# Account of engine time in a scheduled kernel: a task is ready when its predecessor has ended, new first values, one ScalarE square fewer, another order at the end

## The chip, the cores and the metric

The kernel runs on one core of a Trainium2 chip. The metric is the device time of one execution in microseconds (us), as the median of several runs. The engines are named as in the profile: PE (TensorE, matrix products), DVE (VectorE), ACT (ScalarE), POOL (GpSimd), SP (SyncE, which here only starts transfers). Each works through its own instructions in their order and waits on the others by semaphores.

## The reference

Three stages in a row, on 6080 tokens of width 256:

```python
# 1: channel attention; q, k, v are 6080 x 256
s = (k / norm(k)).T @ (q / norm(q)) / tau      # 256 x 256, norms over the tokens
x = v @ softmax(s)
# 2: a feed-forward layer, d_ff = 2048
x = (relu(x @ moe_w_in) ** 2) @ moe_w_out
# 3: another
h = x @ moe2_w_in
out = (h * clip(h + 3, 0, 6) / 6) @ moe2_w_out
```

The weights arrive as 64-bit floats and are turned into 32-bit ones on the chip.

## The kernel before, in words

**Tiling.** Tokens lie along the free axis, in 6 chunks of about 2 x 508. After the attention scores (to about 55 us) a loop runs over 2 layers (`ph`) x 6 chunks (`c`) x 4 cuts of d_ff (`u`) x 2 halves of a cut (`p`), 96 steps `i` of about 10.3 us each (`step`, called from the loop at the end of the function). A step forms a 2 x 2 block product with seven products M1 to M7 in place of eight (Winograd's form). Operands are split into a rounded part and a rest ("hi" and "lo", tiles `wh`/`wl` for weights, the two halves of `b` for data, of `g` for the activations), so each product is three matmuls of 128 x 128 by about 506 columns.

**PE's order within a step** is fixed by `step`: M1, M2, M5 (nine matmuls), 3 of the previous step's 24 output matmuls (`out_mms`, line 765), M6, 5 more, M7, 6 more, M4, 5 more, M3, and the last 5: 45 matmuls. M1, M6, M7 and M4 add up in one PSUM bank `x`, and between them ScalarE copies the bank out: to `m1` after M1, `u2` after M6, `u3` after M7, and after M4 a relu to `r`. So M6 cannot start before the copy to `m1` is done, M7 not before `u2`, M4 not before `u3`. M3 adds into the bank that DVE has to read for `h22 = u3 + y`, and waits for that. From these come h11, h12, h21, h22; each is squared by DVE (or, for some steps, by ACT: relu and square, table `SQUARED_BY_ACT`), then ACT makes the hi half of `g` and DVE the lo half. h12's square and split (`carry`) run in the next step.

**Work on the side.** In layer 1 the weights of layer 2 are prepared as `tasks`: 64-bit words are converted (`ct`, `cv` by ACT; `ct`, `wblk` by DVE, line 138 the last of four), and a task marked `alone` (`add_in_2`, `part`) splits them: ACT writes the hi part to a staging tile `st`, DVE the lo part, and SP stores both to DRAM. A `lane` prepares the data blocks `b` of the next chunk.

**What sets the order.** PE, SP and POOL run in the order written. For ACT and DVE, from step 8 (`MANUAL_FROM`) on, an account of engine time does it while the program is built: `now` holds a time for PE, ACT and DVE; every emitted instruction adds its cost from a table (`MATMUL`, `WIDE_ACT`, `WIDE_DVE`, ...). Between the fixed parts of a step `fill(act_until, dve_until)` emits those side instructions that by the account start early enough to end by then, the earliest first. `starts` takes a task's first instruction as ready at `t.seen`. That is set when the task is loaded, to PE's time plus `LANDING` (3 us), and again whenever one of its own instructions is emitted. The account runs from the kernel's start: `run_outs` adds to PE's time in the first 8 steps too, where `step`'s fixed work is not charged to ACT and DVE.

**The end.** After the last step 24 output matmuls remain, then copies of four results `y` out of PSUM (`y_done`), the last one cut in halves for ACT and DVE. They are run 12 first (with the two copies that these complete), then `carry` (the last square and split of h12), then the other 12.

Of the kernel before, what the change touches and what calls it, by code (L numbers as in the profile page):

```python
# [8 lines left out]
F32 = mybir.dt.float32  # L9
# [7 lines left out]
P = 128  # L17

HALF = 256
HT = 508  # L20
# [26 lines left out]


MATMUL, SEEN, AFTER = 0.2305, 0.26, 0.12
WIDE_ACT, WIDE_DVE, SCALAR_DVE, HALF_ACT, HALF_DVE = 0.55, 0.6, 0.46, 0.32, 0.31  # L50
LANDING = 3.0
LOAD_AHEAD = (2, 8, 8)
PLAIN = 3
# [6 lines left out]
POPS_2 = (3, 5, 6, 5)  # L60
AW_POPS = (1, 1, 1, 1)
FIRST_POPS = (6, 7, 4, 7)
SQUARED_BY_ACT = ("1", "012", "1", "012", "12", "12", "12", "012")


@with_exitstack
def tile_channel_attention_then_two_ffn(
# [13 lines left out]
    PE, ACT, DVE, SP = nc.tensor, nc.scalar, nc.vector, nc.sync  # L81
# [17 lines left out]
    mp = ctx.enter_context(tc.tile_pool(name="mp", bufs=1))  # L99
# [110 lines left out]
    def run(fs):  # L210
        for f in fs:
            f()


    tasks = []
# [8 lines left out]
    def ensure_loads():  # L224
        for t in tasks[:2]:
            if t.steps is None:
                t.steps, t.since, t.seen = t.load(), done[0], now["PE"] + LANDING
# [16 lines left out]
    now = {"PE": 0.0, "A": 0.0, "D": 0.0}  # L244
    lane_seen, stagings = [0.0], [0.0, 0.0]

    def on(engine, cost, f, waits=False, staging=0):
        f.on, f.waits, f.staging = (engine, cost), waits, staging
        return f

    def spend(engine, cost, ready=0.0):
        now[engine] = max(now[engine], ready) + cost
        return now[engine] + AFTER
# [5 lines left out]
    def spent(f, seen):  # L259
        end = spend(*f.on, starts(f, seen))  # L260
        if f.staging == 2:
            stagings.append(end + LANDING)
        return end
# [6 lines left out]
    def emit(k):  # L270
        t = tasks[k]
        turn[0] = k
        f = t.steps.pop(0)
        f()
        t.seen = spent(f, t.seen)
        done[0] += 1
        if not t.steps:
            finished.add(tasks.pop(k).name)
            turn[0] = 0
            ensure_loads()  # L280

    def background(n=1):
        while n > 0 and tasks:
# [88 lines left out]
    def late(make, fine):  # L372

        got = []
        costs = [("A", WIDE_ACT)] * 2 + [("D", SCALAR_DVE)] * 2 + [("D", WIDE_DVE)] * 2
        if not fine:
            costs = [(e, 2 * cost) for e, cost in costs[::2]]

        def at(i):
            def f():  # L380
                if not got:
                    got.extend(make())
                got[i]()
            return on(*costs[i], f, i in (0, len(costs) // 3))
        return [at(i) for i in range(len(costs))]

    for u in range(NU):
        pool, tag = (gp, "g") if u == 0 else (oop, "oh")
# [182 lines left out]
    with tc.tile_pool(name="qk", bufs=4) as qkp, tc.tile_pool(name="at", bufs=1) as atp:  # L571
# [51 lines left out]
        for i, (wide, j, g) in enumerate(pieces):  # L623
            if i:
                load_piece(i + 3)
            t = loaded[i]
# [151 lines left out]
    def y_done(ph, c, b, e, last=False):  # L778
        start, n = chunks[c]
        if ph == 0 and c not in scratch:  # L780
            scratch[c] = dram.tile([C, 2 * HT], F32, tag="y1", name="y1")
        scale = 1.0 if ph == 0 else 1.0 / 6.0


        if ph == 0 and b == 0 and c == NCHUNK - 1:
            pool, tag, bufs = mp, ("u3", "h22")[e], 1
        else:
            pool, tag, bufs = (mp, "r", 2) if ph == 0 and b == 0 else (yp, "y", 2)
        t = pool.tile([P, HT], F32, tag=tag, name="y", bufs=bufs)
        y = y_ps[ph, c, b, e]  # L790
        dst = scratch[c][:, b * n:] if ph == 0 else outT[:, start + b * n:]
        dst = dst[e * P:(e + 1) * P]
        cuts = (0, n // 2, n) if last else (0, n)
        for k, (i, j) in enumerate(zip(cuts, cuts[1:])):
            if k:
                DVE.tensor_scalar(out=t[:, i:j], in0=y[:, i:j], scalar1=scale, scalar2=None, op0=ALU.mult)
            else:
                ACT.activation(out=t[:, i:j], in_=y[:, i:j], func=AF.Copy, scale=scale)
            spend("A", WIDE_ACT, now["PE"] + SEEN)
            (nc.gpsimd if ph == 0 else ACT if last and not k else SP).dma_start(out=dst[:, i:j], in_=t[:, i:j])  # L800

    def run_outs(outs, n):
        for _ in range(min(n, len(outs))):
            f, done = outs.pop(0)
            f()
            now["PE"] += MATMUL
            if done:
                y_done(*done)

    def step(i, ph, c, u, p, before, outs, carry):  # L810
# [35 lines left out]
        def act(h, b):  # L846
            if i < len(SQUARED_BY_ACT) and b in SQUARED_BY_ACT[i]:
                r = tmp("r", 2)
                ACT.activation(out=r, in_=h, func=AF.Relu)
                ACT.activation(out=h, in_=r, func=AF.Square)  # L850
            elif ph == 0:
                DVE.scalar_tensor_tensor(out=h, in0=h, scalar=0.0, in1=h, op0=ALU.max, op1=ALU.mult)  # L852
            else:
                r = tmp("r", 2)
                DVE.tensor_scalar(out=r, in0=h, scalar1=3.0, scalar2=0.0, op0=ALU.add, op1=ALU.max)  # L855
                DVE.scalar_tensor_tensor(out=h, in0=r, scalar=6.0, in1=h, op0=ALU.min, op1=ALU.mult)  # L856

        def relu2(h, x, k):
            r = tmp("r", 2)
            ACT.activation(out=r, in_=x, func=AF.Relu)  # L860
            if str(k) in SQUARED_BY_ACT[i]:
                ACT.activation(out=h, in_=r, func=AF.Square)
# [232 lines left out]
    for i, (ph, c, u, p) in enumerate(order):  # L1095
        at = i % (LAST + 1)
        nxt = (ph, c + 1) if c + 1 < NCHUNK else (1, 0) if ph == 0 else None
        if ph == 0 and c == 0:
            if i == 0:
                add_out_1(1, 3)  # L1100
            elif p == 1 and u + 1 < NU and u:
                add_out_1(u + 1, i + 2)
        if i == 1:
            need(("half o", 0))
            last_lo[2] = last_lo[0].ins
            held.extend([("s", 0), ("w", 0, 1)])
        if (ph, c) == (0, 1) and at == 0:
            end = i + 2
            for x, f in [(x, f) for x in range(NU) for f in (add_in_2, add_out_2)]:
                end += DUE[f is add_out_2]  # L1110
                f(x, end)
        if nxt and at == (2 if i > LAST else 6):
            add_lane(*nxt, FIRST if i > LAST else FIRST + REST, i - at + LAST + (i <= LAST))
        if at == 0:
            assert not lane
        if ph == 0:
            need(("w", ph, u))
            if PLAIN <= u and c == 0:
                need(("t", 0, 0))
            if c == 1 and u < PLAIN:  # L1120
                need(("s", u))
        outs = []
        if not prev:
            need(("w1", 1))
            take = take_next
            outs = [(f, None) for f in ahead[1:]]
        else:
            if prev[0][0] == 0 and prev[0][1] == 0:
                if i > 1:
                    need(("o", prev[0][2]))  # L1130
            outs = out_mms(*prev[0], prev[1])
        if i == MANUAL_FROM:
            phase[0] = 2
            ctx.enter_context(tc.manual_schedule())

        if nxt and at == LAST < i:
            add_lane(*nxt, REST, i + 1)
        g, carry = step(i, ph, c, u, p, before, outs, carry)
        if i == 1:
            first_hi = last_lo[1]  # L1140
        before = []
        if nxt and at == (0 if i > LAST else 5):
            if i <= LAST:
                need(("t", 0, 0))
            load_data(*nxt)
        if ph == 0 and c == 0 and p == 0 and u + 1 < NU:
            need(("w1", u + 1))
            if u:
                if u + 1 == SPLIT_FROM:
                    with tc.issue_after(first_hi), tc.issue_after(last_lo[2]):  # L1150
                        split_e()
                products, before = attn_w(u + 1)
                run(products)
            else:
                before = take
            add_task(("w", 0, u + 1), lambda x=u + 1: in_1_steps(x), i + 2)
        if ph == 0 and c == 0 and u < PLAIN:
            if p == 0 and u == PLAIN - 1 < NU - 1:
                add_data("t", 0, 0, ("sums", 5, 4, 3, 6), i + 2)
            elif p == (u < NU - 1):  # L1160
                add_weight_sums(u, SUMS_DUE[u])
        if ph == 0 and c == NCHUNK - 1 and p:
            fetch_2("w", u)
        if prev and prev[0][0] == 0 and prev[0][1] == NCHUNK - 1 and prev[0][3]:
            fetch_2("o", prev[0][2])
        prev = ((ph, c, u, p), g)
    outs = out_mms(*prev[0], prev[1])
    run_outs(outs, 12)
    run(carry)
    while outs:  # L1170
        f, done = outs.pop(0)
# [33 lines left out]
```

## Time and profile before

| | |
|---|---|
| median of 3 runs | 1078.86 us (1077.34 to 1079.47) |
| the profiled execution | 1078.93 us |
| its span, first to last instruction | 1077.1 us |
| PE busy | 1063.6 us, 99% of the span |
| DVE, ACT busy | 894.5 us (83%), 650.6 us (60%) |
| granted TensorE clock, mean | 0.996 of full |

The profile is of one execution. A busy PE says little here, since matmuls overlap: one of 128 x 506 is listed with 0.39 us while the next starts 0.23 us after it. The time that PE loses is read from the distance between the starts of matmuls, and from idle time with the name of what ended it.

### The profile page before, as it was taken

What the parts mean: (1) busy time and instruction counts of PE and PEld (TensorE: products, weight loads), DVE (VectorE), ACT (ScalarE), POOL (GpSimd) and SP (SyncE); (2) the same over time, 40 slices, a digit from 0 to 9 for tenths busy, and PEclk for the clock granted to TensorE, in tenths of its full rate; (3) what the DMA queues carried; (4) which work ended last, traced back from release to release, by engine and by line L of the source; (5) the groups of instructions that cost most, each with busy time, mean ns of one, the idle gap of its engine ahead of it and who ended that gap; (6) DMA issues with size and microseconds to landing.
All of it is one profiled execution on the core that took longest, in us unless ns stands there. A gap on an engine that the chain in (4) does not pass through costs nothing.

```text
span 1077.1 us, 12850 instructions
## 1 busy us (share of the span) xinstructions
PE 1063.6 (99%) x4602; PEld 867.0 (80%) x4602; DVE 894.5 (83%) x1520; ACT 650.6 (60%) x1129; POOL 22.7 (2%) x46
## 2 busy tenths in 40 slices
PE   9999999899999999999999999999999999999998
PEld 8778878788888878887888888888888888888886
DVE  6899887787887877887887888988888898898785
ACT  7698876566566557567655455555555555555443
POOL 0000000000000000001011000000000000000000
PEclk9999999999999999999999999999999999999999
DMA  9633220123023103115545002002001001000001
GB/s 361 241 97 98 78 97 1 49 84 132 27 89 109 55 34 136 49 50 163 198 167 184 0 1 78 1 1 78 1 1 57 21 1 46 32 1 31 9 1 39
DMA packets 31648, 78.03 MB, mean 72 GB/s; under 512 B 3296, under 2 KB 13792, under 8 KB 31584
## 3 DMA queue, kind: packets, MB, share of 16 engines
q1 hardware_dynamic: 27024, 57.49, 15.9%
q0 software_dynamic: 3840, 17.76, 4.7%
q10 hardware_dynamic: 720, 1.96, 0.5%
q8 instruction: 36, 0.59, 0.2%
q14 instruction: 28, 0.23, 0.1%
HBM read 53.22 MB, written 23.99 MB: 72 GB/s over the span
## 4 chain that ended last, share of the span: by engine, by line
PE 94%; DVE 3%; ACT 1%; DMA 1%; issue 0%; ACTq 0%; DVEq 0%
PE y L765 48%; PE s L825 42%; PE sc L613 4%; DVE g L115 1%; DMA q<-q_dram 1%; DVE b L115 1%; PE s L543 1%; DVE h L118 0%; DVE h L852 0%; DVE ct L146 0%; ACT st L112 0%; ACT u L112 0%; DVE wblk L138 0%; DVE ct L134 0%; ACT wh L112 0%
## 5 line engine op out<-in xcount | busy, mean ns | idle before, releaser
L765 PE MATMUL y<-g,oh 128*128 128x506 f32 (+1 forms) x1536 | 510.5, 394 | 0.0
L825 PE MATMUL s<-b,wh 128*128 128x506 f32 (+1 forms) x1356 | 422.9, 393 | 7.1 <-ACT u L112 5.6
L115 DVE TENSOR_TENSOR g<-h,g 128x506 fp32r<-128x506 f32 (+1 forms) x384 | 261.8, 682 | 99.1 <-ACT g L112 60.1
L765 PEld LDWEIGHTS y<-g,oh 128*128 128x128 f32 x1536 | 290.5, 189 | 64.7 <-DVE g L115 0.4
L825 PEld LDWEIGHTS s<-b,wh 128*128 128x128 f32 x1356 | 254.9, 189 | 68.0 <-ACT u L112 7.6
L765 PE MATMUL y<-g,ol 128*128 128x506 f32 (+1 forms) x768 | 302.8, 394 | 0.0
L825 PE MATMUL s<-b,wl 128*128 128x506 f32 (+1 forms) x678 | 266.5, 393 | 0.2 <-DVE wl L115 0.2
L112 ACT ACTIVATE g<-h 128x506 fp32r<-128x506 f32 (+1 forms) x384 | 235.1, 622 | 26.1 <-DVE h L873 11.0
L112 ACT ACTIVATE u<-s 128x506 f32<-128x506 f32 (+1 forms) x180 | 107.0, 594 | 153.8 <-PE s L825 152.8
L765 PEld LDWEIGHTS y<-g,ol 128*128 128x128 f32 x768 | 145.2, 189 | 32.0
L825 PEld LDWEIGHTS s<-b,wl 128*128 128x128 f32 x678 | 128.1, 189 | 29.2 <-DVE wl L115 1.1
L118 DVE TENSOR_TENSOR h<-u,s 128x506 f32<-128x506 f32 (+1 forms) x180 | 122.1, 678 | 29.5 <-ACT u L112 29.3
L856 DVE SCALAR_TENSOR_TENSOR h<-r,h 128x506 f32<-128x506 f32 (+1 forms) x144 | 98.9, 687 | 4.9
L112 ACT ACTIVATE m<-s 128x506 f32<-128x506 f32 (+1 forms) x90 | 53.3, 592 | 71.4 <-PE s L825 70.6
L852 DVE SCALAR_TENSOR_TENSOR h<-h 128x506 f32<-128x506 f32 (+1 forms) x121 | 82.6, 682 | 1.4
L872 ACT ACTIVATE r<-s,three 128x506 f32<-128x506 f32 (+1 forms) x48 | 32.9, 686 | 65.1 <-PE s L825 65.1
L118 DVE TENSOR_TENSOR h<-m,s 128x506 f32<-128x506 f32 (+1 forms) x90 | 61.0, 678 | 4.8 <-ACT m L112 1.8
L855 DVE TENSOR_SCALAR r<-h 128x506 f32<-128x506 f32 (+1 forms) x144 | 60.6, 421 | 1.7
L112 ACT ACTIVATE b<-blk 128x506 fp32r<-128x506 f32 (+1 forms) x85 | 51.5, 616 | 14.8 <-PE s L825 14.6
L115 DVE TENSOR_TENSOR b<-blk,b 128x506 fp32r<-128x506 f32 (+1 forms) x85 | 57.6, 681 | 1.4 <-ACT b L112 0.9
L869 ACT ACTIVATE r<-s 128x506 f32<-128x506 f32 (+1 forms) x42 | 24.9, 594 | 47.4 <-PE s L825 47.3
L873 DVE SCALAR_TENSOR_TENSOR h<-r,s 128x506 f32<-128x506 f32 (+1 forms) x48 | 32.8, 683 | 14.3 <-ACT r L872 14.3
(97 smaller groups left out, 524.0 us busy)
## 6 DMA issues: line engine op xcount, KB each, us to landing
w<-w_in_dram SPq DMA_DIRECT2D x16, 512.0 KB, 4.5
w<-w_out_dram SPq DMA_DIRECT2D x16, 512.0 KB, 3.8
k<-k_dram SPq DMA_DIRECT2D x10, 512.0 KB, 7.1
blk<-vT_dram SPq DMA_DIRECT2D x8, 506.0 KB, 5.0
y<-y POOLq DMA_DIRECT2D x16, 253.0 KB, 3.3
blk<-y SPq DMA_DIRECT2D x8, 506.0 KB, 4.7
outT_dram<-y SPq DMA_DIRECT2D x15, 253.0 KB, 2.1
q<-q_dram SPq DMA_DIRECT2D x7, 512.0 KB, 7.6
```

The lines of the kernel that those rows point to most:

```text
L112: return ACT.activation(out=out, in_=in_, func=AF.Copy)
L115: return DVE.tensor_tensor(out=out, in0=a, in1=b, op=ALU.subtract)
L118: return DVE.tensor_tensor(out=out, in0=a, in1=b, op=ALU.add)
L613: return lambda: PE.matmul(s_ps[dh][:, :C], t["k"][:, b, dh * P:(dh + 1) * P], t["q"][:, b], start=first, stop=last)
L765: PE.matmul(y_ps[ph, c, b, e][:, :n], w[:, j, e * P:(e + 1) * P], x, start=start, stop=stop)
L825: PE.matmul(dst, w[:, a, rows], x, start=first and k == 0, stop=k == 2, skip_group_check=True)
L852: DVE.scalar_tensor_tensor(out=h, in0=h, scalar=0.0, in1=h, op0=ALU.max, op1=ALU.mult)
L855: DVE.tensor_scalar(out=r, in0=h, scalar1=3.0, scalar2=0.0, op0=ALU.add, op1=ALU.max)
L856: DVE.scalar_tensor_tensor(out=h, in0=r, scalar=6.0, in1=h, op0=ALU.min, op1=ALU.mult)
L869: ACT.activation(out=r, in_=x, func=AF.Relu)
L872: ACT.activation(out=r, in_=x, func=AF.Relu, bias=three)
L873: DVE.scalar_tensor_tensor(out=h, in0=r, scalar=6.0, in1=x, op0=ALU.min, op1=ALU.mult)
```

## The change

Four edits to what sets the order, and one tile:

- `emit`: when a task's last instruction has been emitted, the first task in the list that is marked `alone` becomes ready no earlier than that instruction's end (`x.seen`). Also the first two instructions of a conversion are charged 0.58 each (`SCALAR_ACT`) in place of 0.55.
- At step 8 the account's values are set anew: PE 0, ACT 0.3, DVE 1.0; the times of lane, staging tiles and tasks to 0.
- In step 7 ACT no longer squares block "0" (h12); DVE does.
- At the end `carry` comes before all 24 output matmuls.
- In `y_done` the DVE half of the last result is written to a tile of its own (tag `m1`).

```diff
-WIDE_ACT, WIDE_DVE, SCALAR_DVE, HALF_ACT, HALF_DVE = 0.55, 0.6, 0.46, 0.32, 0.31
+WIDE_ACT, SCALAR_ACT, WIDE_DVE, SCALAR_DVE, HALF_ACT, HALF_DVE = 0.55, 0.58, 0.6, 0.46, 0.32, 0.31
...
-SQUARED_BY_ACT = ("1", "012", "1", "012", "12", "12", "12", "012")
+SQUARED_BY_ACT = ("1", "012", "1", "012", "12", "12", "12", "12")
...
             finished.add(tasks.pop(k).name)
             turn[0] = 0
             ensure_loads()
+            for x in tasks:
+                if x.alone:
+                    x.seen = max(x.seen, t.seen)
+                    break
...
-        costs = [("A", WIDE_ACT)] * 2 + [("D", SCALAR_DVE)] * 2 + [("D", WIDE_DVE)] * 2
+        costs = [("A", SCALAR_ACT)] * 2 + [("D", SCALAR_DVE)] * 2 + [("D", WIDE_DVE)] * 2
...
             if k:
+                t = mp.tile([P, HT], F32, tag="m1", name="y")
                 DVE.tensor_scalar(out=t[:, i:j], in0=y[:, i:j], scalar1=scale, scalar2=None, op0=ALU.mult)
...
         if i == MANUAL_FROM:
             phase[0] = 2
+            now.update(PE=0.0, A=0.3, D=1.0)
+            lane_seen[0] = 0.0
+            stagings[:] = [0.0, 0.0]
+            for t in tasks:
+                t.seen = 0.0
             ctx.enter_context(tc.manual_schedule())
...
     outs = out_mms(*prev[0], prev[1])
-    run_outs(outs, 12)
     run(carry)
```

In the built program the instructions of PE, SP and POOL stand in the same order as before. ACT's and DVE's differ at eight places; ACT has two instructions fewer, DVE one more.

**ACT at about 200 us** (step 13). `st<-wblk` is the hi part of a converted block of layer 2's weights. Before:

```order
L112 ACTIVATE m1_1870<-s_1873 128x508
L112 ACTIVATE g_1884<-h12_1779 128x508
L112 ACTIVATE b_1886<-blk_1507 128x506
L112 ACTIVATE st_1907<-wblk_1699 128x512
L112 ACTIVATE u2_1871<-s_1873 128x508
L112 ACTIVATE g_1910<-h11_1866 128x508
L112 ACTIVATE u3_1872<-s_1873 128x508
```

After:

```order
L112 ACTIVATE m1_1868<-s_1871 128x508
L112 ACTIVATE g_1882<-h12_1777 128x508
L112 ACTIVATE b_1884<-blk_1505 128x506
L112 ACTIVATE u2_1869<-s_1871 128x508
L112 ACTIVATE g_1906<-h11_1864 128x508
L112 ACTIVATE u3_1870<-s_1871 128x508
L112 ACTIVATE st_1929<-wblk_1697 128x512
```

`st` moved from ahead of the copy to `u2` to behind the copy to `u3`. At about 383 us the same happens in the same words. At about 290 and 485 us `st` stood between `u3` and `r`, and now stands behind the first of the two `g` that follow. At about 301 us the half-size `st` moved from ahead of `m1` to ahead of `u3`; at about 370 us `cv`, at about 458 us `ct` and `cv` moved from ahead of `u2` to behind the `g` after it (that last `cv` to behind `u3`). DVE's order changed at 147, 290 to 302 and 460 us alone.

**ACT and DVE at about 147 us** (steps 7 and 8). `wh` and `wl` are splits of weight sums. ACT before:

```order
L112 ACTIVATE g_1379<-h21_1291 128x508
L849 ACTIVATE r_1418<-h12_1290 128x508
L850 ACTIVATE h12_1290<-r_1418 128x508
L112 ACTIVATE wh_588<-wblk_456 128x512 x2
L112 ACTIVATE m1_1411<-s_1414 128x508
L112 ACTIVATE g_1432<-h12_1290 128x508
L112 ACTIVATE u2_1412<-s_1414 128x508
```

ACT after:

```order
L112 ACTIVATE g_1379<-h21_1291 128x508
L112 ACTIVATE wh_588<-wblk_456 128x512
L112 ACTIVATE m1_1411<-s_1414 128x508
L112 ACTIVATE g_1425<-h12_1290 128x508
L112 ACTIVATE u2_1412<-s_1414 128x508
L112 ACTIVATE g_1442<-h11_1407 128x508
L112 ACTIVATE wh_588<-wblk_456 128x512
L112 ACTIVATE u3_1413<-s_1414 128x508
```

DVE after (before, the square, line 857 here, of h12 was not there, and the two `wl` stood ahead of `h11<-m1`):

```order
L115 TENSOR_TENSOR g_1365<-h22_1292,g_1365 128x508
L115 TENSOR_TENSOR g_1379<-h21_1291,g_1379 128x508
L857 SCALAR_TENSOR_TENSOR h12_1290<-h12_1290 128x508
L118 TENSOR_TENSOR h11_1407<-m1_1411,s_1421 128x508
L115 TENSOR_TENSOR g_1425<-h12_1290,g_1425 128x508
L857 SCALAR_TENSOR_TENSOR h11_1407<-h11_1407 128x508
L115 TENSOR_TENSOR wl_589<-wblk_456,wh_588 128x512 x2
L115 TENSOR_TENSOR g_1442<-h11_1407,g_1442 128x508
```

The relu and square of h12 are gone from ACT, and one DVE square took their place; one `wh` and both `wl` moved behind work on h11.

**The end**, with the semaphores that are waited for. ACT before:

```order
L112 ACTIVATE g<-h_9371 128x506 [waits DVE_49]
L112 ACTIVATE g<-h_9370 128x506 [waits DVE_49]
L798 ACTIVATE y<-y 128x506 [waits DMAHW7_49,PE_49]
L798 ACTIVATE y<-y 128x506 [waits DMAHW0_49,PE_49]
L112 ACTIVATE g<-h_9369 128x506 [waits DVE_49]
L798 ACTIVATE y<-y 128x506 [waits DMAHW1_49,PE_49,Activation_49]
L798 ACTIVATE y<-y 128x253 [waits DMAHW2_49,PE_49,Activation_49]
```

ACT after:

```order
L112 ACTIVATE g<-h_9369 128x506 [waits DVE_49]
L112 ACTIVATE g<-h_9368 128x506 [waits DVE_49]
L112 ACTIVATE g<-h_9367 128x506 [waits DVE_49,PE_49]
L803 ACTIVATE y<-y 128x506 [waits DMAHW7_49,PE_49]
L803 ACTIVATE y<-y 128x506 [waits DMAHW0_49,PE_49]
L803 ACTIVATE y<-y 128x506 [waits DMAHW1_49,PE_49,Activation_49]
L803 ACTIVATE y<-y 128x253 [waits DMAHW2_49,PE_49,Activation_49]
```

DVE after:

```order
L115 TENSOR_TENSOR g<-h_9368,g 128x506 [waits Activation_49]
L860 TENSOR_SCALAR r<-h_9367 128x506 [waits DVE_49]
L861 SCALAR_TENSOR_TENSOR h_9367<-r,h_9367 128x506 [waits DVE_49]
L115 TENSOR_TENSOR g<-h_9367,g 128x506 [waits Activation_49]
L801 TENSOR_SCALAR y<-y 128x253 [waits Activation_49]
```

The hi part of h12 moved ahead of all four copies of `y`. DVE's half of the last copy waits for ACT alone, before also for five transfers.

## Rows read from the trace of the kernel before

**Rows 1.** The page: span; busy us (share of the span) xinstructions of each engine.

```profile
span 1077.1 us, 12850 instructions
...
PE 1063.6 (99%) x4602; PEld 867.0 (80%) x4602; DVE 894.5 (83%) x1520; ACT 650.6 (60%) x1129; POOL 22.7 (2%) x46
```

**Rows 2.** Who waited for whom on PE: total us, times, longest.

```profile
PE s L825 <- ACT u L112: 5.6, 3, 2.7
```

**Rows 3.** The chain that ended last: start, us, what; an undisturbed stretch.

```profile
829.41 2.06 PE s L825 x9
```

**Rows 4.** By stretch: length, busy (x) by engine, PEclk, DMA share, GB/s.

```profile
202.49:205.57 3.08, 0.38 (x2) 0.00 (x0) 1.82 (x4) 1.16 (x3) 0.00 (x0) 1.00 0.00 0
205.57:209.31 3.74, 3.73 (x9) 2.95 (x10) 2.28 (x4) 1.06 (x2) 0.00 (x0) 0.54 0.19 70
383.23:386.18 2.95, 0.40 (x2) 0.00 (x0) 1.69 (x3) 1.16 (x3) 0.00 (x0) 1.00 0.00 0
386.18:390.12 3.94, 3.94 (x10) 3.14 (x11) 2.65 (x4) 1.06 (x2) 0.00 (x0) 0.57 0.18 67
491.05:491.79 0.74, 0.39 (x2) 0.00 (x0) 0.74 (x2) 0.69 (x2) 0.00 (x0) 1.00 0.05 19
```

**Rows 5.** ACT in order of time: start, us, line, out<-in [idle before <-releaser].

```profile
204.41 0.63 ACT L112 ACTIVATE st<-wblk 128x512 fp32r<-128x512 f32 x1 [3.62 <-DVE wblk L138]
```

**Rows 6.** DVE in order of time, the same stretch.

```profile
201.91 0.68 DVE L115 TENSOR_TENSOR b<-blk,b 128x506 fp32r<-128x506 f32 x1
202.51 0.42 DVE L134 TENSOR_SCALAR ct<-ct 128x512 uint32<-128x512 uint32 x1
...
203.69 0.69 DVE L138 SCALAR_TENSOR_TENSOR wblk<-w,ct 128x512 uint32<-128x512 uint32 x1
```

**Rows 7.** ACT in order of time, at 383 us.

```profile
385.02 0.63 ACT L112 ACTIVATE st<-wblk 128x512 fp32r<-128x512 f32 x1 [4.00 <-DVE wblk L138]
```

**Rows 8.** ACT in order of time, at 491 us.

```profile
485.50 0.63 ACT L112 ACTIVATE st<-wblk 128x512 fp32r<-128x512 f32 x1 [3.05 <-DVE wblk L138]
...
490.33 0.63 ACT L112 ACTIVATE g<-h 128x506 fp32r<-128x506 f32 x1 [1.54 <-DVE h L852]
490.86 0.40 ACT L112 ACTIVATE st<-wblk 128x256 fp32r<-128x256 f32 x1
```

**Rows 9.** PE in order of time, at 147 us.

```profile
147.16 0.40 PE L765 MATMUL y<-g,oh 128*128 128x508 f32 x1
149.01 0.72 PE L825 MATMUL s<-b,wh 128*128 128x508 f32 x2 [1.45 <-ACT m L112]
```

**Rows 10.** ACT in order of time, at 147 us.

```profile
144.78 1.14 ACT L112 ACTIVATE g<-h 128x508 fp32r<-128x508 f32 x2
...
147.34 1.13 ACT L112 ACTIVATE wh<-wblk 128x512 fp32r<-128x512 f32 x2
148.38 0.57 ACT L112 ACTIVATE m<-s 128x508 f32<-128x508 f32 x1
```

**Rows 11.** DVE in order of time, at 147 us.

```profile
146.03 1.28 DVE L115 TENSOR_TENSOR g<-h,g 128x508 fp32r<-128x508 f32 x2
```

**Rows 12.** All engines in order of time, at the end.

```profile
1068.99 1.28 ACT L798 ACTIVATE y<-y 128x506 f32<-128x506 f32 x2 [2.92 <-PE y L765]
...
1070.17 0.62 ACT L112 ACTIVATE g<-h 128x506 fp32r<-128x506 f32 x1
...
1070.62 0.71 PE L765 MATMUL y<-g,oh 128*128 128x506 f32 x2
1070.82 0.69 DVE L115 TENSOR_TENSOR g<-h,g 128x506 fp32r<-128x506 f32 x1 [2.57 <-ACT g L112]
...
1072.14 1.08 ACT L798 ACTIVATE y<-y 128x506 f32<-128x506 f32 x2 [1.35 <-PE y L765]
1072.35 0.40 PE L765 MATMUL y<-g,oh 128*128 128x506 f32 x1
...
1073.25 0.42 DVE L796 TENSOR_SCALAR y<-y 128x253 f32<-128x253 f32 x1 [1.75 <-ACT y L798]
```

## The prediction

> **What bounds the kernel now.** I read the page first: PE is busy for 99% of the span, DVE for 83%, ACT for 60% [rows 1]. PE's program is the same after the change, so the time can fall only by what PE loses between matmuls, and rise only by new losses. The chain of waits gives the undisturbed pace: nine matmuls in 2.06 us, 0.229 each [rows 3]; I use 0.23. Against this pace I read the starts of PE's matmuls through the whole trace. After 60 us there are five places with a distance well over 0.23, and four of them are waits for ACT's copies out of PSUM, which the list of waits puts at 5.6 us for the `u` copies [rows 2] and at 1.45 for one `m1` [rows 9]. The reader should see in each place who made ACT late: ACT is not overloaded, it stands. At 200 us it idled 3.62 us for a converted block, `wblk`, and the copy to `u2`, whose input lay ready, was queued behind that [rows 5]. At 383 us it was the same with 4.00 us [rows 7].
>
> **The five losses of before, priced.**
>
> *200 us.* From the matmul at 202.49 to the next start 3.08 us passed; 0.23 would do: 2.85 lost. Behind the wait the granted clock was 0.54 (mostly the lower level, 1.2 of 2.4 GHz) and nine matmuls took 3.74 us in place of 9 x 0.23 = 2.07: 1.67 more [rows 4]. Together 4.52.
>
> *383 us.* 2.95 - 0.23 = 2.72, then ten matmuls in 3.94 at 0.57, in place of 2.30: 1.64. Together 4.36 [rows 4].
>
> *147 us.* From 147.16 to 149.01 are 1.85, so 1.62 lost, and the next two matmuls took 0.72 where one distance and one length would be 0.23 + 0.39 = 0.62: 0.10. Together 1.72 [rows 9].
>
> *491 us.* 0.74 - 0.23 = 0.51 [rows 4], and again some 0.10 behind it: 0.61.
>
> *The end.* From 1070.62 to 1072.35 six distances of 0.23 would be 1.38; they took 1.73: 0.35 [rows 12].
>
> All five: 11.56 us.
>
> **The change part by part.**
>
> *`st` behind `u3` (200 and 383 us).* The matmul that stood was M7's first, due at 202.49 + 0.23 = 202.72. M6 ended six starts and one length earlier, at 202.72 - 1.38 + 0.39 = 201.73. ACT, which no longer stands, copies to `u2` from then for some 0.6, to 202.4: before M7 is due. So the wait goes. What is late next? The conversion has not moved on DVE: `b` at 201.91, then the last three of the four conversion steps to 203.69 + 0.69 = 204.38 [rows 6], and behind them the lo part of h11 (one DVE place, 0.60 by the distance of the first two of [rows 6]) and the sum for h22 (0.68). That ends at 205.66. M3 waits for it, and is due 3 + 6 + 3 + 5 = 17 matmuls after M7's first, at 206.63: 0.97 to spare. `st` itself starts at 204.41, as before, and ends at 205.04; the relu behind it needs M4's end, M7's start plus 11 x 0.23 + 0.39 = 205.64. Nothing waits. At 383 us the same sum with M7 due at 383.46: `wblk` done by 385.02, h22 by 386.3, M3 due at 387.37, 1.1 to spare. I take back all of 4.52 and 4.36; without that cover a microsecond of lateness would cost one. Lower bound 4.0 and 3.9, if each hand-over adds half a microsecond to a chain that I have read as back to back.
>
> *`st` behind a `g` (290 and 485 us).* At 485.50 ACT had stood 3.05 us, with the relu after M4 behind `st`. M7 was due at 491.28, its predecessor 45 matmuls earlier, at 480.93, so M4's end was at 480.93 + 2.53 + 0.39 = 483.85 and the relu could have started some 2 us sooner. That delay went through g, DVE's lo parts and the square of h12 to the ACT instruction at 490.33, which idled 1.54 us for that square, and the half-size `st` at 490.86 behind it then made `u2` late [rows 8]. Only 0.51 is needed there, so I take back the 0.61; lower bound 0.2. At 290 us no matmul was late, and I count nothing. What `st` now holds up there is the hi part of h21. It is wanted first by the next step's seventh output matmul, 18 matmuls or 4.1 us into that step, which covers it.
>
> *One square less on ACT, `wh` and `wl` later (147 us).* ACT ends its two g at 144.78 + 1.14 = 145.92 [rows 10]. Then comes one `wh` (some 0.57, half of 1.13) and the copy to `m1` (0.57) [rows 10]: done at 147.1, and M6 is due at 147.16 + 0.23 = 147.39. So this wait goes too. But DVE now squares h12 behind its two lo parts, from 147.31 - 0.09 to about 147.9 [rows 11], ACT splits it to 148.6, copies `u2` to 149.1 (M7 is due at 147.39 + 8 x 0.23 = 149.23), DVE brings the lo part of h12 and the square of h11 to 149.9, ACT splits that to 150.55, does the second `wh` to 151.0 and only then `u3`, to 151.6. M4 is due 17 matmuls after M6, at 151.30, so a new wait of 0.3 appears. I take 0.3 (0 if ACT's overlap hides it, 0.7 if each of the four hand-overs between ACT and DVE costs 0.1). Net 1.4, between 1.0 and 1.72. The square that DVE takes over costs 0.6 to 0.7 once, on an engine that stands for 17% of the span; the wait of 0.3 is its price.
>
> *Conversions at 301, 370 and 458 us.* No wait of PE lies there; ACT's copies to `u2` get earlier and the moved instructions stand where ACT idles. Nothing, between -0.3 and 0.3 in all.
>
> *The end.* DVE had idled 2.57 us before 1070.82, so the square of h12 was done at 1068.25; ACT idled 2.92 before its first copy of `y` at 1068.99, and only behind two copies, at 1070.17, split h12 [rows 12]. Now it splits h12 from 1068.3 to 1068.9, and DVE follows to 1069.6. The output matmuls that need the two parts stand at 1070.6 and later, and the first copy of `y` still starts at 1068.99. So 0.35 comes back (bounds 0 and 0.35).
>
> The tile of its own for DVE's half is worth nothing by the order: DVE's last instruction waits for ACT and for no PE semaphore, though it reads what PE wrote; so the wait must be for an ACT instruction that itself waited for PE, which is ACT's copy of the same bank. In the trace before DVE's half began at 1073.25, when ACT's copies (1072.14 + 1.08) had ended [rows 12], and it will again. The Trainium skill, PSUM — Partial Sum Buffer, section "PSUM bank collisions raise a hardware error", says why a separate tile does not help: two engines may not read one bank at once, even in different columns, so the two halves have to be ordered. By it this edit brings 0, as I count; if the halves did overlap, it would bring up to the 0.42 of DVE's half.
>
> **Sum.** 4.52 + 4.36 + 0.61 + 1.4 + 0.35 = 11.24. The profiled execution took 1078.93 (span 1077.1, 1.83 around it), which is 0.07 over the median of 1078.86. 1078.93 - 11.24 = 1067.69, against the median 1067.6. With all lower bounds the gain is 4.0 + 3.9 + 0.2 + 1.0 + 0 - 0.3 = 8.8 (1070.1), with all upper ones 11.56 + 0.3 + 0.42 = 12.3 (1066.6).
>
> **The rivals.**
>
> *h22 takes the place of `u2`.* The conversion still stands on DVE ahead of the sum for h22, on which M3 waits. For it: at 200 and 383 us DVE works without a gap up to the block's end. Against: 0.97 and 1.1 to spare. It decides once this sum ends over 1 us later than I have it. A wait of 1 us at both places gives 1069.6; one of over 2.5 at one of them brings the lower clock back as well, and so about 4.4 [rows 4]: 1072.
>
> *The conversion is what is late, and the order only chooses who waits.* One mechanism at all four `st`: the block comes so late that what now stands behind `st` (the relu, or h21's hi part) is late for PE. Then each place costs what 200 and 383 us cost, some 4.45, so 17.8 in place of the 9.5 that three of them cost before, and with the other gains (1.75) the time is 1078.9 + 17.8 - 9.5 - 1.75 = 1085.4. It decides when `wblk` ends some 4 us after its present place for h21, 0.6 for the relu to be late at all. Against: 204.38 is known, and DVE's instructions before it are not delayed by anything that moved.
>
> *The change does not do what it says.* The tail's tile has no effect (counted). If the waits were not ACT's order but DVE's conversion itself ending late for PE by another path, nothing would change: 1078.9.
>
> **How the numbers follow.** The forecast with its bounds gets 0.86, h22 in place of `u2` 0.09, nothing gained 0.03, the late conversion 0.02. The time is that of the forecast, 1067.6. Runs of one kernel lay 1.5 below and 0.6 above the median before. The range takes the bounds 1066.6 to 1070.1, widened below by 0.6 and above by 0.9 for that scatter and for the milder half of the first rival: 1066.0 to 1071.0. A difference under 0.2% (2.2 us) cannot be told from none. Faster by more: 0.95; within: 0.03; slower: 0.02.
>
> **What would show it.** In the changed kernel's profile I expect: no wait of PE for a `u` copy over 0.4 us and no stretch after 60 us, before the end, with a granted clock under 1; `st` at about 200 us starting within 0.1 us of its `wblk` while PE runs on; at about 151 us a wait of some 0.3 for `u3`; at the end the split of h12 ahead of the copies and DVE's half starting when ACT's has ended. The list of PE's waits for `u` copies should fall from 5.6 us to under 0.5. The prediction is wrong if a wait for `h` from DVE or for `r` appears at the `st` places, or if lower clock remains without a wait before it.

## The result and the profile after

| | before | after |
|---|---|---|
| median of 5 runs | 1077.99 us (1077.34 to 1079.47) | 1067.85 us (1067.69 to 1068.04) |
| the profiled execution | 1078.93 us | 1068.04 us |
| its span | 1077.1 us | 1066.3 us |

The ratio is 0.9903, with an interval of 0.9889 to 0.9918: 0.97% faster. The forecast was 1067.6, in a range of 1066.0 to 1071.0. The profiled execution became 10.9 us shorter, the median 10.1; the difference between these two is taken up under the experiments, with the clock.

The page of after, which answers [rows 1] (span; busy us, share of the span, instructions):

```profile
span 1066.3 us, 12846 instructions
...
PE 1060.2 (99%) x4602; PEld 865.6 (81%) x4602; DVE 894.2 (84%) x1521; ACT 650.0 (61%) x1127; POOL 22.6 (2%) x46
```

PE has the same 4602 matmuls and its busy time fell by 3.4 us. Nearly all of this, 1.67 + 1.64 = 3.31, is what the two stretches of [rows 4] at the lower clock took over the undisturbed pace. The list of PE's waits in after, whole (total us, times, longest; `s` at L582 and `sc` at L617 lie in the start-up):

```profile
PE s L582 <- DVE ones L517: 1.1, 1, 1.1
PE sc L617 <- DMA q<-q_dram: 0.4, 1, 0.4
PE s L830 <- DVE wl L115: 0.2, 1, 0.2
```

The 5.6 us for `u` copies of [rows 2] and the 1.45 for `m1` of [rows 9] are gone, and no `h` or `r` stands in their place. Line 825 of before is line 830 now.

**200 and 383 us.** By stretch (length, busy us (xmatmuls) of PE first, then PEld, DVE, ACT, POOL; granted clock, DMA share, GB/s). These four lie at the places of the first four of [rows 4] and have about their lengths:

```profile
202.50:205.57 3.07, 3.07 (x15) 2.48 (x14) 3.00 (x6) 1.91 (x4) 0.00 (x0) 1.00 0.15 58
205.57:209.31 3.74, 3.74 (x18) 3.05 (x17) 3.15 (x6) 3.00 (x6) 0.00 (x0) 1.00 0.35 128
383.20:386.20 3.00, 3.00 (x15) 2.48 (x14) 2.83 (x6) 1.61 (x5) 0.00 (x0) 1.00 0.16 61
386.18:390.12 3.94, 3.94 (x19) 3.25 (x18) 3.87 (x8) 2.81 (x5) 0.00 (x0) 1.00 0.17 57
```

Two matmuls in 3 us became 15. Nine in 3.74 us at a clock of 0.54 became 18 at 1.00, and ten in 3.94 us became 19. ACT and DVE of after in order of time at 200 us, each engine apart (start, us, what, in brackets the idle time before it and what ended it), with the PE row of M3 last:

```profile
200.94 0.60 ACT L112 ACTIVATE u<-s 128x508 f32<-128x508 f32 x1 [0.98 <-PE s L830]
...
203.59 0.63 ACT L112 ACTIVATE st<-wblk 128x512 fp32r<-128x512 f32 x1 [0.21 <-DVE wblk L138]
...
202.87 0.69 DVE L138 SCALAR_TENSOR_TENSOR wblk<-w,ct 128x512 uint32<-128x512 uint32 x1
...
204.07 0.68 DVE L118 TENSOR_TENSOR h<-u,s 128x508 f32<-128x508 f32 x1
...
205.81 0.62 PE L830 MATMUL s<-b,wh 128*128 128x508 f32 x2
```

`st` no longer stands 3.62 us [rows 5] with `u2` behind it: `u2` waits for PE alone, and `st` starts 0.03 us after `wblk` has ended (202.87 + 0.69 = 203.56). The sum for h22 ends at 204.75, and M3 starts at 205.81: 1.06 us to spare.

**147 us.** PE, ACT and DVE of after, each in order of time, at the place of [rows 9 to 11]:

```profile
151.57 0.39 PE L769 MATMUL y<-g,ol 128*128 128x508 f32 x1
152.10 0.72 PE L830 MATMUL s<-b,wh 128*128 128x508 f32 x2
...
146.83 0.58 ACT L112 ACTIVATE m<-s 128x508 f32<-128x508 f32 x1
...
150.41 0.63 ACT L112 ACTIVATE g<-h 128x508 fp32r<-128x508 f32 x1 [0.87 <-DVE h L857]
150.95 0.61 ACT L112 ACTIVATE wh<-wblk 128x512 fp32r<-128x512 f32 x1
151.47 0.57 ACT L112 ACTIVATE u<-s 128x508 f32<-128x508 f32 x1
...
149.70 0.68 DVE L857 SCALAR_TENSOR_TENSOR h<-h 128x508 f32<-128x508 f32 x1
```

`m1` is done at 147.41, and M6 starts at 147.89, in time. The new wait stands before M4: the copy to `u3` ends at 152.04, and from 151.57 to 152.10 are 0.53 where 0.23 would do: M4 is 0.30 late. ACT's 150.41 stands for DVE's square of h11 (0.87), and the second `wh` lies between it and `u3`.

**The end.** ACT, DVE and PE of after, which answer [rows 12]:

```profile
1057.98 0.63 ACT L112 ACTIVATE g<-h 128x506 fp32r<-128x506 f32 x1 [2.27 <-DVE h L861]
1058.63 1.28 ACT L803 ACTIVATE y<-y 128x506 f32<-128x506 f32 x2
1061.43 1.07 ACT L803 ACTIVATE y<-y 128x506 f32<-128x506 f32 x2 [1.51 <-PE y L769]
...
1062.53 0.42 DVE L801 TENSOR_SCALAR y<-y 128x253 f32<-128x253 f32 x1 [3.20 <-ACT y L803]
...
1061.41 0.39 PE L769 MATMUL y<-g,ol 128*128 128x506 f32 x1
1061.64 0.39 PE L769 MATMUL y<-g,oh 128*128 128x506 f32 x1
```

The split of h12 comes first, PE's last matmuls follow one another at 0.23 (the last two: 1061.41 and 1061.64), and DVE's half of the last result starts 0.03 us after ACT's copies have ended (1061.43 + 1.07 = 1062.50), as in before.

### The profile page after: what moved, and what is told of

Its sections match the earlier page's. It is cut to its first block, busy times and chain, and to the rows that moved or that the text cites. A ratio compares the mean times of both kernels' runs of the same rounds, so it can differ in the third digit from the quotient of the medians.

```text
span 1066.3 us, 12846 instructions
## 1 busy us (share of the span) xinstructions
PE 1060.2 (99%) x4602; PEld 865.6 (81%) x4602; DVE 894.2 (84%) x1521; ACT 650.0 (61%) x1127; POOL 22.6 (2%) x46
## 4 chain that ended last, share of the span: by engine, by line
PE 97%; DVE 1%; DMA 1%; ACT 0%; issue 0%; ACTq 0%
PE y L769 49%; PE s L830 43%; PE sc L617 4%; DMA q<-q_dram 1%; PE s L547 1%; DVE b L115 0%; DVE g L115 0%; ACT g L112 0%; DVE h L857 0%; DVE wl L115 0%; ACT u L112 0%; ACT wh L112 0%; PE aw L543 0%; PE s L669 0%; DVE ct L134 0%
## 5 line engine op out<-in xcount | busy, mean ns | idle before, releaser
L112 ACT ACTIVATE g<-h 128x506 fp32r<-128x506 f32 (+1 forms) x384 | 235.4, 623 | 25.2 <-DVE h L878 11.2
```

The lines of the kernel that those rows point to most:

```text
L112: return ACT.activation(out=out, in_=in_, func=AF.Copy)
```

## The experiments

My theory: the gain is a sum of places. At each, ACT stood for a block that was not yet converted (or did work too early), and behind it was a copy that PE wanted; at the two longest waits the lower clock came on top. The main rival: the late conversion only passes its wait on, to h22. All kernels compute the whole result; the two with extra DVE instructions add them on a tile of their own.

**One edit alone, and all but it.** The kernel before with the edit of `emit` only:

```diff
             turn[0] = 0
             ensure_loads()
+            for x in tasks:
+                if x.alone:
+                    x.seen = max(x.seen, t.seen)
+                    break
```

> The kernel before, with the one edit that makes a task marked alone ready no earlier than the end of the task before it. It moves st, at 200 and 383 us, and the half-size st, ct and cv elsewhere; the order at 147 us and at the end stays as before. Theory (each PE loss belongs to one place in ACT's order): the losses at 200, 383 and 491 us go (4.56 + 4.39 + 0.60 = 9.5 us), those at 147 us (1.7) and the end (0.35) stay: 1078.0 - 9.5 = 1068.5 us. Rival (the edits work together: ACT's lighter load and the new first values are needed for st to be harmless): over 1071 us, with waits of PE at other places. Rival (the lower clock at 200 and 383 us is not a consequence of the waits): about 1071.7, with a clock under 1 left there.

Measured: 1069.87 us (1069.62 to 1070.25), ratio 0.9917 (0.9901 to 0.9934). Of PE's waits after the start-up one is left over 0.2 us:

```profile
PE s L829 <- ACT m L112: 1.5, 1, 1.5
```

And the changed kernel without that edit:

```diff
             turn[0] = 0
             ensure_loads()
-            for x in tasks:
-                if x.alone:
-                    x.seen = max(x.seen, t.seen)
-                    break
```

> The changed kernel without that one edit. Theory: the waits of about 2.85 and 2.7 us and the lower clock behind them come back at 200 and 383 us, and 0.6 at 491 us; only 147 us and the end are better than before: 1067.9 + 9.5 = 1077.4 us, within 0.1% of the kernel before. Rival (edits work together): 1070 to 1075 us.

Measured: 1076.79 us (1075.82 to 1078.26), ratio 0.9985 (0.9976 to 0.9994). The stretches of [rows 4] are back (columns as there):

```profile
201.28:204.37 3.09, 0.39 (x3) 0.00 (x1) 1.82 (x4) 1.17 (x3) 0.00 (x0) 1.00 0.00 0
204.37:208.11 3.74, 3.74 (x10) 2.96 (x11) 2.33 (x4) 1.06 (x2) 0.00 (x0) 0.54 0.19 70
382.02:384.97 2.95, 0.40 (x2) 0.00 (x1) 1.69 (x3) 1.16 (x3) 0.00 (x0) 1.00 0.00 0
384.97:388.91 3.94, 3.94 (x11) 3.14 (x12) 2.66 (x4) 1.05 (x2) 0.00 (x0) 0.58 0.18 67
```

So this edit alone carries 200, 383 and 491 us, and nothing else touches them. Counted by the starts of PE's matmuls, the kernel with this edit only loses 1.31 us against the changed kernel at 147 us and 0.35 at the end, and nothing at the other three places. The new charge of 0.58 for conversions is not in that kernel; without it one `cv` at about 370 us keeps its old place on ACT, and PE loses nothing there either.

Both expected times missed, the first by 1.4 us too low, the second by 0.6 too high, and for one reason: I took the two stretches at the lower clock, as the profiled execution has them, to lie in every run. The ten runs of the kernel without the edit lie in two groups, five at 1075.8 to 1076.1 (mean granted clock 0.998) and five at 1077.5 to 1078.3 (0.996 to 0.997). The kernel before does the same: of its 13 runs beside these, six lie at 1079.1 to 1079.3 (0.996 to 0.997) and five at 1077.4 to 1077.7 (0.998), two between. The groups are 1.6 us apart for the kernel before, which is what one stretch at the lower clock costs [rows 4], and 1.9 for the other. The traces fit: those with a mean of 0.996 (before, this one, and the square alone below) have two such stretches, the one with 0.998 (the first values alone, below) has one.

**How early may `st` stand?** The changed kernel, with the task's ready time 1.8 us earlier:

```diff
-                    x.seen = max(x.seen, t.seen)
+                    x.seen = max(x.seen, t.seen - 1.8)
```

> The changed kernel, with the time at which the split becomes ready put 1.8 us too early. At 200 and 383 us st then stands one copy earlier, between the g of h11 and the copy to u3; at 290 and 485 us between u3 and the relu, as in the kernel before. Theory (a copy behind st is late by what the conversion is late, worked out from starts): at 200 us wblk ends at 203.56, st at 204.2, u3 at 204.7 with M4 due at 203.97: a wait of 0.8 and 0.1 behind it; the same at 383 us (wblk ends 379.61, u3 380.7, M4 due 380.2 or so): 0.6 to 0.8; 0.6 at 491 us. No lower clock, since the wait of 1.45 us in the kernel before left it at 1. Sum 2.0 to 2.5: 1069.9 to 1070.4 us. Rival (any standing of ACT for st brings the lower clock): 1073 us or more.

Measured: 1070.88 us (1070.24 to 1071.51), ratio 0.9927 (0.9913 to 0.9942). PE, then ACT:

```profile
203.31 0.39 PE L769 MATMUL y<-g,ol 128*128 128x508 f32 x1
204.34 0.73 PE L830 MATMUL s<-b,wh 128*128 128x508 f32 x2 [0.64 <-ACT u L112]
...
203.17 0.63 ACT L112 ACTIVATE st<-wblk 128x512 fp32r<-128x512 f32 x1 [1.54 <-DVE wblk L138]
203.71 0.57 ACT L112 ACTIVATE u<-s 128x508 f32<-128x508 f32 x1
```

`st` now stands ahead of `u3` and makes M4 late in place of M7, by 1.03 - 0.23 = 0.80 here and by 0.67 at 380 us. At 482 us it is M7 again that is late, by 0.53: there `st` stands ahead of the relu, and the half-size `st` behind it is late for `u2`, as [rows 8] show for the kernel before. With 0.10 behind each wait that is 2.3 us over the changed kernel; the median lies 3.0 over it, the profiled run (1070.24) 2.2 over the profiled run there. The clock stayed at 1.00 through all three waits. The mechanism holds: a task that stands one place too early on ACT costs PE what is left of ACT's idle time. What made the other runs up to 1.3 longer than the profiled one was not traced.

**The place at 147 us, edit by edit.** The kernel before with each of the two edits that act there, one run each:

```diff
-SQUARED_BY_ACT = ("1", "012", "1", "012", "12", "12", "12", "012")
+SQUARED_BY_ACT = ("1", "012", "1", "012", "12", "12", "12", "12")
```

> The kernel before, with h12 of step 7 squared by DVE in place of ACT, and nothing else. At 147 us ACT then has two wh between its second g and the copy to m1. Theory: ACT's g end at 145.9 (in the time of the trace before), two wh take 1.1, m1 0.57: done at 147.5 with M6 due at 147.39: a wait of 0.15 to 0.3 in place of 1.62, and M4 not late, since the second wh no longer stands ahead of u3: the place gains 1.3 to 1.5, about what the whole change gains there (1.3). Rival (the place needs the later wh): the wait at M6 stays over 0.7.

```diff
             phase[0] = 2
+            now.update(PE=0.0, A=0.3, D=1.0)
+            lane_seen[0] = 0.0
+            stagings[:] = [0.0, 0.0]
+            for t in tasks:
+                t.seen = 0.0
```

> The kernel before, with the account's new first values at step 8 alone: the second wh stands behind the g of h11, the relu and square of h12 still on ACT. Theory: m1 starts one wh sooner, at 147.86 in place of 148.38, so the wait at M6 falls from 1.62 to 1.1; what stands ahead of u3 then makes M4 late by 0 to 0.4. The place gains 0.1 to 0.5 us, so the square is the edit that matters there. Rival (the first values matter): over 1 us.

Measured: 1079.35 and 1078.00 us, beside 1079.34 for the kernel before; what counts is the place. With the square alone M6 is late by 0.10 only, but M4 by 0.57. PE, ACT and DVE of that kernel:

```profile
152.51 0.40 PE L765 MATMUL y<-g,ol 128*128 128x508 f32 x1
153.31 0.74 PE L825 MATMUL s<-b,wh 128*128 128x508 f32 x2 [0.40 <-ACT u L112]
...
152.15 0.63 ACT L112 ACTIVATE g<-h 128x508 fp32r<-128x508 f32 x1 [1.85 <-DVE h L852]
152.68 0.58 ACT L112 ACTIVATE u<-s 128x508 f32<-128x508 f32 x1
...
149.04 1.29 DVE L115 TENSOR_TENSOR wl<-wblk,wh 128x512 fp32r<-128x512 f32 x2
150.25 0.68 DVE L118 TENSOR_TENSOR h<-m,s 128x508 f32<-128x508 f32 x1
```

The two `wl` stand on DVE ahead of h11, so h11's square comes late, ACT stands 1.85 us for it, and `u3` is queued behind. I had expected M4 in time there and a gain of 1.3 to 1.5: missed. With some 0.1 behind each of the two waits the place loses 0.88 in place of 1.72, a gain of 0.84. The first values alone move one `wh` and both `wl`: M6 comes 1.10 late, with 0.10 behind it 1.2 in place of 1.72, a gain of 0.51, at the upper end of what I expected. So the square is worth more, but not nearly all. Together they give 1.35, and the changed kernel gains 1.3 there. The two edits add up: by the orders shown, one frees ACT ahead of `m1` and the other frees both engines ahead of h11.

**The end as before.** The changed kernel with the order of the end and the tile undone, one run:

```diff
-                t = mp.tile([P, HT], F32, tag="m1", name="y")
                 DVE.tensor_scalar(out=t[:, i:j], in0=y[:, i:j], scalar1=scale, scalar2=None, op0=ALU.mult)
...
+    run_outs(outs, 12)
     run(carry)
```

> The changed kernel, with the end as before: 12 output matmuls and two copies of y ahead of the last split of h12, and DVE's half of the last copy in the tile that ACT writes. Theory: PE's last matmuls lose 0.35 us again (distances of 0.3 to 0.4 in three places), ACT's split of h12 starts behind two copies; DVE's half starts within 0.1 us of the end of ACT's half in both kernels, so the tile of its own is worth nothing. Rival (the tile frees DVE's half): DVE's half starts 0.3 us or more later, counted from the end of ACT's copies, than in the changed kernel.

Measured: 1068.85 us. Three distances between PE's last matmuls are 0.32, 0.39 and 0.33 again, 0.35 over three of 0.23. PE at the longest of them, then ACT and DVE:

```profile
1060.98 0.40 PE L769 MATMUL y<-g,ol 128*128 128x506 f32 x1
1061.37 0.72 PE L769 MATMUL y<-g,oh 128*128 128x506 f32 x2
...
1061.95 1.08 ACT L802 ACTIVATE y<-y 128x506 f32<-128x506 f32 x2 [1.35 <-PE y L769]
...
1063.06 0.42 DVE L800 TENSOR_SCALAR y<-y 128x253 f32<-128x253 f32 x1 [1.74 <-ACT y L802]
```

DVE's half starts 0.03 us after ACT's end without the tile too: the place of `carry` is worth the 0.35, the tile nothing.

**The rival that h22 takes over.** The changed kernel with small DVE instructions (0.45 us each) ahead of the sum for h22, in the two steps:

```diff
+EXTRA = {13: 2, 30: 4}
...
+            for _ in range(EXTRA.get(i, 0)):
+                sub(extra, extra, extra)
```

> The changed kernel, with extra DVE instructions (128 x 256, some 0.43 us each, on a tile of their own) right ahead of the sum for h22: two in step 13 (about 200 us), four in step 30 (about 383 us). They show how near the first rival of the prediction was, in which the sum for h22 becomes late for M3. Theory (the changed trace has M3 start 1.06 us after this sum at 200 us, 1.21 at 383 us): two cost 0.9 and no wait of PE; four cost 1.75 and a wait of M3 of 0.5 to 0.7, for DVE's h, and no lower clock. Rival (DVE has more room than one step's margin): no wait at either. Rival (no room at all): 0.9 and 1.8 us.

Measured: 1068.66 us, one run. Two of them (0.88 us) at 200 us cost nothing; M3 starts at 205.71 after a sum that ends at 205.45. Four at 380 us, DVE and then PE:

```profile
380.04 1.80 DVE L116 TENSOR_TENSOR extra<-extra 128x256 f32<-128x256 f32 x4
381.76 0.68 DVE L119 TENSOR_TENSOR h<-u,s 128x506 f32<-128x506 f32 x1
...
382.50 0.73 PE L833 MATMUL s<-b,wh 128*128 128x506 f32 x2 [0.41 <-DVE h L119]
```

M3 becomes 0.57 late, 0.68 with what lies behind. In after the sum starts at 380.13 and ends 1.21 us ahead of M3; PE itself runs 0.09 earlier in this run. So the sum was moved by 381.76 - 380.13 + 0.09 = 1.72. That is 0.51 more than the margin, and 0.06 pass from the end of the sum to M3's start: 0.57. The rival's mechanism is real; in the changed kernel the sum is not late enough for it.

**The lower clock.** In the one run with the first values alone the second long wait did not bring it (length, PE first, then the granted clock, as above):

```profile
203.12:206.21 3.09, 0.39 (x2) 0.00 (x0) 1.83 (x4) 1.16 (x3) 0.00 (x0) 1.00 0.00 0
206.21:209.95 3.74, 3.74 (x12) 2.98 (x13) 2.66 (x4) 1.06 (x2) 0.00 (x0) 0.69 0.19 70
383.84:386.79 2.95, 0.40 (x2) 0.00 (x0) 1.69 (x3) 1.16 (x3) 0.00 (x0) 1.00 0.00 0
386.79:390.73 3.94, 3.94 (x17) 3.25 (x18) 2.65 (x4) 1.87 (x4) 0.00 (x0) 1.00 0.18 67
```

So the changed kernel was given other waits of such lengths, for another engine, by more of the same extra instructions, and run beside the changed kernel itself:

```diff
-EXTRA = {13: 2, 30: 4}
+EXTRA = {13: 7, 30: 9}
```

> The changed kernel with more of the extra DVE instructions ahead of the sum for h22, to make PE wait longer: seven in step 13, nine in step 30. By the margins and prices of the run with two and four (0.45 each, 1.06 and 1.2 us to spare) M3 waits 2.0 us at 200 us and 2.8 us at 383 us. It shows when the lower clock follows a wait. Theory one (it follows a wait of over 2.5 us in every run): a clock of 0.5 for 3.4 us after the second wait in every run, none after the first: 1067.9 + 2.1 + 2.9 + 1.7 = 1074.6 us, all runs alike. Theory two (a wait of this length brings it in some runs and not in others, as one of the runs shown had a wait of 2.55 us without it): two groups of runs 1.7 us apart, about 1072.9 and 1074.6.

> The changed kernel once more, on the same chip as the next run, so that the two can be compared: 1067.7 to 1068.1 us.

Measured: 1075.09 us (six runs; five at 1074.59 to 1075.31, one at 1076.23), ratio 0.9968 (0.9957 to 0.998). The changed kernel beside it: 1068.59 us (1068.26 to 1070.82), ratio 0.9913 (0.9898 to 0.9928). The waits of the first:

```profile
205.33:207.65 2.32, 0.40 (x2) 0.00 (x0) 2.18 (x6) 0.53 (x1) 0.00 (x0) 1.00 0.10 36
207.65:211.39 3.74, 3.74 (x16) 3.10 (x17) 3.65 (x7) 2.57 (x5) 0.00 (x0) 1.00 0.29 105
383.73:386.83 3.10, 0.40 (x2) 0.00 (x1) 2.89 (x8) 0.53 (x1) 0.00 (x0) 1.00 0.02 7
...
388.15:391.50 3.35, 3.35 (x9) 2.65 (x8) 2.47 (x4) 1.11 (x4) 0.00 (x0) 0.51 0.22 81
```

A wait of 1.93 us (the first stretch less PE's 0.40) left the clock at 1.00; one of 2.71 was followed by a stretch at the lower clock, which began 1.2 us after PE had started again. No run of this kernel has a mean clock over 0.998, and none lies in a group 1.6 below the others, so the wait of 2.71 seems to have brought the lower clock each time, as theory one has it, though one trace alone shows it. With 2.32 + 3.10 - 0.46 = 4.96 of lateness, some 0.25 behind it and 1.6 for the clock, 6.8 on the changed kernel's 1068.4 (its three undisturbed runs here) gives 1075.2. All four runs of the changed kernel lie above the 1067.7 to 1068.1 that I expected. Of the 0.8 by which its traced run here is longer than the first, 0.4 lie in the start-up and 0.3 behind PE's last matmul. Two runs stay unexplained, both without a trace: this kernel's 1076.23 (0.996) and the changed kernel's 1070.82 (0.998, the others 0.999 and 1.0). By these means each may hold one stretch more at the lower clock; no trace shows it.

**A version that beats both.** The wait of 147 us that is left goes if the account's first value for DVE is later, since the second `wh` then comes behind `u3`; and the last copy need not be cut if its halves run one behind the other anyway:

```diff
-        cuts = (0, n // 2, n) if last else (0, n)
+        cuts = (0, n)
...
-            now.update(PE=0.0, A=0.3, D=1.0)
+            now.update(PE=0.0, A=0.3, D=2.2)
```

> The changed kernel with DVE's first value in the account 2.2 in place of 1.0, which puts the second wh (and its wl) behind u3 and two copies of y, and with the last result copied whole by ACT in place of half by ACT and half by DVE. Theory: the remaining wait at 152 us (0.3 and 0.1 behind it) goes, since u3 then ends at 151.5 with M4 due at 151.8; at the end ACT's whole copy ends about 0.3 us sooner than DVE's half, which starts only when ACT's half has ended, and one transfer of 253 KB lands no later than the second of two of 126 KB: 0.4 + 0.3 = 0.7 less, 1067.2 us. Rival (the halves pay by their earlier first transfer): the end is 0 to 0.3 longer and the sum 1067.5 to 1067.8.

> The version with the second wh behind u3 and the whole last copy, beside the changed kernel. Theory (0.4 us at 152 us and about 0.15 at the end are gone, as its trace showed): 0.4 to 0.7 us under the changed kernel, all runs of it under all runs of that. Rival (chips and placement made the difference between the earlier sets of runs): within 0.2 us.

Measured: 1067.28 us (1067.17 to 1067.54), ratio 0.9894 (0.988 to 0.9909), and beside the changed kernel 1067.15 us (1066.98 to 1067.56) against 1068.59 (1068.26 to 1070.82). PE, then ACT:

```profile
151.39 0.39 PE L769 MATMUL y<-g,ol 128*128 128x508 f32 x1
151.62 0.62 PE L830 MATMUL s<-b,wh 128*128 128x508 f32 x2
...
150.77 0.58 ACT L112 ACTIVATE u<-s 128x508 f32<-128x508 f32 x1
```

M4 starts 0.23 after its predecessor: the 0.40 is back. The last copy ends 1.07 us after PE's last start in place of 1.31, so cutting it cost 0.24. From PE's last start to the end of the span the two kernels, run side by side, took 4.96 (changed) and 4.34 us (this one), 0.6 less; by the first pair of traces it is 0.2 less, and the changed kernel's own two traces differ by 0.33 there. So what the whole copy is worth beyond the 0.24 stays open. Side by side the medians differ by 1.4 us, more than the 0.4 to 0.7 that I expected: of the 1.66 between the two traced runs 0.58 lie in the start-up, which this version does not touch.

## Why the prediction was right, point by point

- **The two long waits, 4.52 and 4.36 predicted.** Places before less places after give 4.56 and 4.39. The cover was as reckoned: 0.97 and 1.1 to spare for h22 against 1.06 and 1.21 in the trace, and the extra DVE work showed that PE waits once this margin is used up. So the rival was a real mechanism, and its condition (over 1 us later) was right; the change does not meet it.
- **491 us, 0.61:** 0.60. In after this step lies at about 480 us. ACT's `g` at 478.44 no longer stands for the square of h12 (1.54 us in [rows 8]), so the half-size `st` behind it, which still comes ahead of `u2`, is done early, and `u2` at 480.55 waits for PE alone.
- **147 us, net 1.4:** 1.3. The old loss of 1.72 went as read. The new wait was found where I put it: `u3` ends 4.15 us after M6's start (4.2 in my sum), and M4 is 0.30 late. What I left out is that the matmuls behind a wait lose another 0.10, which I had counted for the old wait and not for the new one: 0.40 in place of 0.3. The experiment on the square alone missed for another reason: there I had not followed DVE's order (`wl` ahead of h11) as I did for the whole change.
- **The end, 0.35:** 0.35, and the tile 0. Here the reading of the wait was the right one. The Trainium skill, PSUM — Partial Sum Buffer, section "PSUM bank collisions raise a hardware error", has it that two engines may not read the same partitions of one bank at once, whatever the columns. The traces agree as far as they go: with the tile and without it DVE's half began 0.03 us after ACT's.
- **The sum, 11.24:** by places 11.2. PE's last start moved by 1072.35 - 1061.64 = 10.71 only, since in the profiled execution of after everything behind the start-up lies 0.5 later: the score matmuls that wait for a load of q start at 7.81 us in place of 7.27. This start-up differs between executions (0.58 us between the traces of the changed kernel and the last version, run side by side), and the orders changed only from 147 us on.
- **What failed is a step that the forecast didn't have.** I set 1078.93, with its two stretches at the lower clock, beside the median, and took it for the typical run. By their times and mean clocks about half of the runs before have only one such stretch, and the median of five is 1077.99. Against those the gain is some 9.8, against the others 11.3; the medians differ by 10.1, where I forecast 11.2. The time came out right all the same, and not by luck: a stretch that the profiled execution had stood both in the time that I started from and in the sum that I took off. After the change there is no such stretch in any traced run, so that little is left to vary; the one run of 1070.82 may be an exception.

## What to carry to other kernels

Where an engine that feeds PE idles and a copy out of PSUM is queued behind what it idles for, price the place by the distance between PE's starts, with the clock behind it, and then follow each engine that is now next for one step: the margin found so (1 us for h22) can be tested by adding work until it is gone. An account that orders instructions has to know when a predecessor ends; 1.8 us too early in it put the wait back on the next copy here. Look at the clocks of all runs before you set one profiled execution beside a median.

## What the runs showed of the hardware

- One kernel's runs can differ by one stretch at the lower clock (1.2 of 2.4 GHz, some 3.4 us, price 1.6 us). Waits of PE of 0.4 to 1.9 us were never followed by it in the traces here. Of the two waits of 2.7 and 2.55 us in the kernel before and in its kin, the first was followed by it in all four traces read (before, all but `emit`, the square alone, the first values alone), the second in three of them. Why it follows in one run and not in another stays open.
- In all eight stretches that the traces show in mid-kernel, the lower clock came only after PE had started again, 0.1 to 1.4 us later, and then stayed for 3.4 us, with PE at work all the time. In the run with the first values alone it came 1.4 us late, so its stretch of 3.74 us shows 0.69 and 12 matmuls where [rows 4] show 0.54 and nine.
- DVE and ACT start a next instruction before the one ahead is listed as ended (DVE: 0.60 us from start to start where 0.68 is listed, [rows 6]; ACT: two `wh` listed with 1.13 and the next start after 1.04, [rows 10]). So a margin added up from listed durations comes out too small: I counted the listed 0.69 for `wblk`, where the next instruction started 0.61 after it (in after, 202.87 to 203.48), and got 0.97 in place of 1.06.
